# Weights decoded with a scaled copy on ScalarE in place of cleared signs, their factor of two taken out in later steps, and the whole order of steps written anew

## Chip, core and metric

One core of a Trainium2 chip. The metric is the time of one execution of the program in device microseconds; the table below gives the median of the runs shown. Shares of TensorE's clock are shares of 2.4 GHz.

## What is computed

A Nystrom attention of 4 batches with 8 heads (576 positions, 32 landmarks), whose output (2304 tokens by 512) goes through two feed-forward layers:

```
A, Bm, C = softmaxes of q, k and their landmark means
Z = six Newton steps on Bm
x = (A @ Z @ C @ v), heads side by side          # 2304 x 512
h = x @ moe_w_in;  x = (h * tanh(softplus(h))) @ moe_w_out
h = x @ moe2_w_in; x = relu(h) ** 2 @ moe2_w_out
```

All inputs are 4-byte words. As the kernel reads the four weight matrices, each value is a pair of words (`raw` has the shape 128 x 512 x 2): `low` is the lower word of an 8-byte float, `up` the upper one, and the kernel puts a 4-byte float together from them.

## The kernel before, in words

**Order.** The kernel is one long list of steps, `PROGRAM` (2560 steps). A step is `thing.step`, for example `U17.ab`: step `ab` of weight unit 17. The list is walked once and each step issues its instructions; nothing reorders them afterwards, so on every engine and on the queue of SyncE (SP), which issues all transfers, instructions stand in the order of the list. Between engines a tile framework puts the waits, from the order of the list: an instruction waits for earlier steps of the list that use the same tile.

**Weights.** 64 units (`U0` to `U63`, class `Unit`), each a tile of 128 x 512 pairs. Units 0 to 31 are layer 1, 32 to 63 layer 2. The steps of a unit: `d` loads it, `lo` makes a small number of the lower word (ScalarE, L325), `st` puts the sign of the upper word on it (VectorE, L328), `ab` clears the sign of the upper word (L335 on ScalarE for units 0 to 15, L337 on VectorE for units 16 to 63), `cl` clamps and shifts the upper word (VectorE, L341 and L342), `ad` adds both words as integers (GpSimd), `hi` and `lw` split the result in a high and a low part.

**Attention.** Groups `a` to `h` (two for each batch) with small TensorE steps (`tq`, `tk`, `pa`, `pb`, `pc`, `pe`, `pv`), reductions on VectorE (`sq`, `sk`, `cm`, `am`, `su`), exponentials on ScalarE (`ce`, `ae`), and the Newton steps `B0` to `B2` (`be`, `bs`, `n0` to `n5`, `r`, `z`). The steps `F` fold the attention's small matrices into the first weights: `fo` (TensorE, L826), `mh` (ScalarE, L834) and `ml` (VectorE, L837).

**Layer 1.** 24 turns `t0` to `t23`: `f` (matmuls into `h`), `M` (Mish on ScalarE, L893), `c` and `g` (high and low part), `y` (matmuls into `y`), `e` (accumulate). Mish and the exponentials need different function tables of ScalarE; the steps `x.m` and `x.e` load them ahead.

**Layer 2.** Three passes over the tokens. Steps `Q` and `K` work with sums and differences of weight blocks; blocks `Y10` to `Y22` do products into tiles `O` (L841 to L843) and `a` adds them to `total` (L1140 on ScalarE, L1143 on VectorE).

**The end.** The last pass ends with the products of `Q26` and `Q27`: step `yk` (k = 0 to 5; 6 matmuls, L1288 to L1290) adds to one half of a two-bank PSUM tile, and step `Z2.ek` reads that half on VectorE, adds `total` (L1189, two instructions) and writes an output tile. `Z2.ok` issues its four transfers on SP (L1195). `Z2.u4`, `u6`, `u7`, `u8` combine totals (L1163).

```
sums[p, k // 2] = big(f"O{p}{k // 2}", ...)     # one tile [2, 512] for k and k + 1
ps = sums[p, k // 2][:, k % 2, :]               # Q.y writes, Z2.e reads this half
```

So `y0` and `y1` share a tile, `y2` and `y3`, and `y4` and `y5`.

Of the kernel before, what the change touches and what calls it, by code (L numbers as in the profile page):

```python
# [29 lines left out]
BOTTOM = 2.0 ** -15  # L30
TOP = 122880.0 - 2.0 ** -7
NW = 24
BESIDE = 64
# [20 lines left out]
    B0.n2@at+2 U3.ab U2.cl f.lk B0.r2 c.Sk c.tl@y B0.z2 U3.cl c.TL d.tk@h a.tb U3.ad a.cv U7.ab b.pv@y+1 d.sk d.lv
    b.ae U2.ad a.ah c.pb@at B0.n3@y+2 c.PB d.Tk c.pc@h U7.cl c.lv B0.r3 d.Sk B0.z3 b.cr U7.ad B0.n4@y c.cm b.cv
    e.tk@h B0.r4 a.al B0.z4 c.ce b.su B0.n5@y d.tl@y d.TL c.pa@at e.lv B0.z5 U7.hi B0.pw@y+3 e.Tk c.at U7.lw d.pb@y
    c.am U5.lo d.pc@at b.mu U4.hi B0.wz d.cm F00.fo@h U4.lw b.tb d.ce e.sq b.ah d.pe@at b.al U8.d F00.mh f.tk@h+4
    f.lv d.PB d.ET F00.ml c.mi U6.lo f.lq d.pa@at B1.bx t0.f0 c.ae d.at B1.be f.Tk U6.st t0.f1 c.su U6.ab t0.f2
    t0.M0 B1.bs t0.f3 d.cr U5.st B1.nr@y t0.M1 B1.rs c.pe@h U8.lo d.pv@y U5.ab d.am B1.n0@y+2 U6.cl f.tq@at B1.z0
    U8.st e.Sq U6.ad d.cv B1.r0 c.ET e.sk B1.n1@y t0.c0 B1.z1 U6.hi B1.r1 t0.g0 e.tq@h B1.n2@y t0.c1 B1.z2 e.Sk d.mi  # L60
    U5.cl B1.r2 U5.ad f.Tq B1.n3@y+4 c.cr c.pv@y e.Tq B1.r3 U5.hi B1.z3 U6.lw B1.n4@y+3 U5.lw c.cv f.sq e.tl@y B1.r4
    e.TL U8.ab B1.z4 f.Sq B1.n5@at B1.z5 t0.g1 e.pc@h U8.cl U8.ad U11.d e.pb@at c.mu d.ae e.PB B1.pw@y B1.wz f.sk
    t0.y0 e.cm f.Sk t0.y1 d.su t0.e0 U11.lo U11.st U9.d f.tl@at f.TL t0.e1 t0.y2 c.tb e.ce f.pa@at f.pc@h F10.fo@h
# [1325 lines left out]
```

## Time and profile before

| | |
|---|---|
| median of 3 runs | 796.35 us (795.89 to 798.09) |
| the profiled execution | 795.44 us |
| its span, first to last instruction | 793.6 us |
| busy: TensorE matmul / VectorE / ScalarE / GpSimd | 764.7 / 588.1 / 367.5 / 384.4 us |
| mean granted TensorE clock | 0.995 |

The span is what the trace shows; 1.84 us of the execution lie around it. A busy TensorE counts overlapped matmuls as one stretch. Step names don't stand in the trace: an instruction there has its line and its tiles, and the step follows from the order of the list (`q26w` and `q27w` are the weights of `Q26` and `Q27`).

### The profile page before, as it was taken

The numbers are of one execution on the slowest core, as the hardware profiler recorded it, in microseconds if no ns is written. First come the engines' busy times: TensorE is split into PE (matmuls) and PEld (weight loads), VectorE is DVE, ScalarE is ACT, GpSimd is POOL, SyncE is SP. The second block draws the span as 40 slices with busy tenths as digits, with TensorE's granted clock in tenths as the row PEclk, the third lists the DMA queues.
The fourth block names the chain that finished last, engine by engine and source line by source line (L and its number), as shares of the span: only waits on it lengthen the run. The fifth ranks groups of instructions, "written<-read, shape, count | busy, mean of one in ns | idle before, by whom it ended". The sixth has DMA issues, their size and how long they took to land.

```text
span 793.6 us, 15301 instructions
## 1 busy us (share of the span) xinstructions
PE 764.7 (96%) x5878; PEld 713.0 (90%) x5878; DVE 588.1 (74%) x937; ACT 367.5 (46%) x582; POOL 384.4 (48%) x273
## 2 busy tenths in 40 slices
PE   5798999999999999999999999999999999999996
PEld 4567989889999999899998988999899999999995
DVE  7998876768557667878777777757776777875883
ACT  5686988744453654556456234240253432232220
POOL 1244445141142543434466657576586587454440
PEclk9999999999999999999999999999999999999999
DMA  9972552223131246564558789888899877779903
GB/s 272 304 202 55 144 172 91 71 54 90 45 99 61 86 171 210 196 232 157 189 207 263 243 276 304 254 269 272 254 289 382 300 251 238 221 217 314 333 33 79
DMA packets 87783, 156.71 MB, mean 197 GB/s; under 512 B 9376, under 2 KB 37024, under 8 KB 87712
## 3 DMA queue, kind: packets, MB, share of 16 engines
q1 hardware_dynamic: 87712, 155.75, 61.9%
q8 instruction: 46, 0.75, 0.4%
q14 instruction: 25, 0.20, 0.1%
HBM read 119.54 MB, written 36.18 MB: 196 GB/s over the span
## 4 chain that ended last, share of the span: by engine, by line
PE 87%; DVE 6%; DMA 2%; ACT 1%; issue 1%; POOL 0%; SPq 0%; DVEq 0%; POOLq 0%; ACTq 0%
PE y L841 8%; PE y L843 8%; PE y L842 8%; PE P L1221 7%; PE P L1222 7%; PE P L1223 7%; PE O L843 4%; PE O L842 4%; PE O L841 4%; PE h L841 4%; PE h L843 4%; PE h L842 4%; PE O L1290 3%; PE O L1289 3%; PE O L1288 3%; PE m L826 2%
## 5 line engine op out<-in xcount | busy, mean ns | idle before, releaser
L1117 POOL TENSOR_TENSOR glr<-A,ghr 128x768 fp32r<-128x768 f32 x49 | 100.1, 2063 | 69.9 <-ACT ghr L1112 69.9
L843 PE MATMUL O<-b,glr 128*128 128x256 f32 x294 | 83.0, 282 | 0.0
L842 PE MATMUL O<-b,ghr 128*128 128x256 f32 x294 | 83.0, 282 | 0.0
L841 PE MATMUL O<-b,ghr 128*128 128x256 f32 x294 | 82.9, 282 | 0.0
L841 PE MATMUL h<-ah,mh 128*128 128x384 f32 (+1 forms) x256 | 78.5, 307 | 0.0
L843 PE MATMUL h<-ah,ml 128*128 128x384 f32 (+1 forms) x256 | 77.9, 304 | 0.0
L842 PE MATMUL h<-al,mh 128*128 128x384 f32 (+1 forms) x256 | 77.9, 304 | 0.0
L955 DVE TENSOR_TENSOR acc<-acc,y 128x384 f32<-128x384 f32 x72 | 39.4, 550 | 51.6 <-PE y L843 51.3
L1112 ACT CAST ghr<-A 128x768 fp32r<-128x768 f32 x49 | 40.1, 837 | 73.8 <-PE O L842 28.0
L1251 DVE TENSOR_TENSOR U<-U,P 128x384 f32<-128x384 f32 x72 | 39.7, 551 | 33.8 <-PE P L1223 32.6
L843 PEld LDWEIGHTS O<-b,glr 128*128 128x128 f32 x294 | 56.1, 191 | 0.0
L842 PEld LDWEIGHTS O<-b,ghr 128*128 128x128 f32 x294 | 56.0, 191 | 0.0
L841 PEld LDWEIGHTS O<-b,ghr 128*128 128x128 f32 x294 | 55.9, 190 | 0.0
L914 DVE TENSOR_TENSOR gl<-s,gh 128x768 fp32r<-128x768 f32 x48 | 48.8, 1019 | 6.8 <-ACT gh L904 6.8
L893 ACT ACTIVATE s<-h 128x768 f32<-128x768 f32 x48 | 38.8, 811 | 31.5 <-PE h L843 21.1
L841 PEld LDWEIGHTS h<-ah,mh 128*128 128x128 f32 x256 | 48.5, 190 | 3.4 <-issue 1.9
L843 PEld LDWEIGHTS h<-ah,ml 128*128 128x128 f32 x256 | 48.6, 190 | 0.0
L842 PEld LDWEIGHTS h<-al,mh 128*128 128x128 f32 x256 | 48.6, 190 | 0.0
L1231 ACT COPY U<-P 128x384 f32<-128x384 f32 x24 | 11.5, 479 | 72.9 <-PE P L1223 70.7
L1251 DVE TENSOR_TENSOR A<-U,P 128x384 f32<-128x384 f32 x56 | 30.2, 549 | 20.1 <-PE P L1223 16.9
L904 ACT CAST gh<-s 128x768 fp32r<-128x768 f32 x48 | 39.7, 835 | 7.2 <-PE y L843 7.0
L348 POOL TENSOR_TENSOR wi<-rawwi 128x512 int32<-128x512 int32 x16 | 18.3, 1145 | 46.7 <-DVE rawwi L342 29.4
(698 smaller groups left out, 2510.2 us busy)
## 6 DMA issues: line engine op xcount, KB each, us to landing
b<-sc SPq DMA_DIRECT2D x98, 256.0 KB, 4.2
rawwo<-in_moe_w_out_dram SPq DMA_DIRECT2D x32, 512.0 KB, 4.2
rawwi<-in_moe_w_in_dram SPq DMA_DIRECT2D x48, 256.0 KB, 4.0
v<-in_v_dram SPq DMA_DIRECT2D x16, 288.0 KB, 7.4
out_dram<-o SPq DMA_DIRECT2D x72, 64.0 KB, 2.7
rawwi<-in_moe_w_in_dram SPq DMA_DIRECT2D x8, 512.0 KB, 4.4
st<-wh SPq DMA_DIRECT2D x8, 512.0 KB, 4.0
st<-ws SPq DMA_DIRECT2D x8, 512.0 KB, 3.0
```

The source lines that it names most:

```text
L841: nc.tensor.matmul(ps, wh, rh, start=start, stop=False)
L842: nc.tensor.matmul(ps, wh, rl, start=False, stop=False)
L843: nc.tensor.matmul(ps, wl, rh, start=False, stop=stop)
L904: nc.scalar.copy(gh, s)
L914: nc.vector.tensor_tensor(self.gl[:, sl, :], self.s[hf], self.gh[:, sl, :].bitcast(F32), ALU.subtract)
L955: nc.vector.tensor_tensor(a, a, ps, ALU.add)
L1112: nc.scalar.copy(self.form(k)[0], self.A[self.src(k)])
L1117: nc.gpsimd.tensor_tensor(lo, self.A[self.src(k)], hi.bitcast(F32), ALU.subtract)
L1221: nc.tensor.matmul(ps[:, :TT], wh[:, c], xh[:, c, :], start=c == 0, stop=False)
L1222: nc.tensor.matmul(ps[:, :TT], wh[:, c], xl[:, c, :], start=False, stop=False)
L1223: nc.tensor.matmul(ps[:, :TT], wl[:, c], xh[:, c, :], start=False, stop=c == 1)
L1251: nc.vector.tensor_tensor(to, x, self.ps[i][:, :TT], ALU.add)
```

## The change

- `ab` becomes one ScalarE instruction for all 64 units: a copy of the upper word, read as a float, times 2^-112. It keeps the sign. The VectorE form (L337) is gone, and so is the sign-clearing function of L335.
- `lo` writes an integer now (scale 2^-29, bias 2^23); `st` is as before; `cl` clamps from above and from below, then shifts, with the same two instructions and other constants.
- The weights come out with a factor of two. It is taken out where a result leaves PSUM: `mh` and `ml` multiply by 0.5; in layer 2 `a`, `f`, `e` multiply by 2^-5. ScalarE copies get a scale; VectorE's two-input adds and subtractions become `scalar_tensor_tensor`, and a VectorE copy becomes a `tensor_scalar`. No instruction is added by that.
- `PROGRAM` has the same 2560 steps in another order from its 54th step on. Its head up to there is the same.

```
 def lo(self):
-    nc.scalar.activation(self.low.bitcast(F32), self.low, AF.Copy, scale=2.0 ** -51, bias=2.0)
+    nc.scalar.activation(self.low.bitcast(I32), self.low, AF.Copy, scale=2.0 ** -29, bias=WHOLE)
 def ab(self):
-    if not self.beside:
-        nc.scalar.activation(self.up.bitcast(F32), self.up.bitcast(F32), AF.Abs)
-    else:
-        nc.vector.tensor_scalar(self.up, self.up, 0x7FFFFFFF, None, ALU.bitwise_and)
+    nc.scalar.activation(self.up.bitcast(F32), self.up.bitcast(F32), AF.Copy, scale=REBIAS)
 def cl(self):
-    nc.vector.tensor_scalar(up.bitcast(F32), up.bitcast(F32), BOTTOM, TOP, ALU.max, ALU.min)
+    nc.vector.tensor_scalar(up.bitcast(F32), up.bitcast(F32), TOP, -TOP, ALU.min, ALU.max)
     nc.vector.tensor_scalar(up, up, 3, None, ALU.logical_shift_left)
 class Fold: mh, ml
-    nc.scalar.copy(self.m[0], self.ps)
+    nc.scalar.activation(self.m[0], self.ps, AF.Copy, scale=0.5)
-    nc.vector.tensor_tensor(self.m[1], self.ps, self.m[0].bitcast(F32), ALU.subtract)
+    nc.vector.scalar_tensor_tensor(self.m[1], self.ps, 0.5, self.m[0].bitcast(F32), ALU.mult, ALU.subtract)
 class Block: a
-    nc.vector.tensor_tensor(t, t, self.ps[k], ALU.add)
+    nc.vector.scalar_tensor_tensor(t, self.ps[k], UNDO, t, ALU.mult, ALU.add)
 class Ending: e
-    nc.vector.tensor_tensor(self.t[h, c][:, ds], x[:, c, :], ps[:, ds], ALU.add)
+    nc.vector.scalar_tensor_tensor(self.t[h, c][:, ds], ps[:, ds], UNDO, x[:, c, :], ALU.mult, ALU.add)
...
 PROGRAM, its end
-    Y22.p5@h Y22.a7 Q26.y4 Q26.y2 (with Q26.h0, Q26.g0, Q27.h0 and others between)
-    Y22.p3@h Z2.u2 Q27.g0 Q27.y4 Z2.u3 Y22.a3 Q26.y0 Q26.y3 Q27.y2 Z2.u7 Q27.y0 Q27.y3 Q26.y1 Z2.u8 Z2.e4 Z2.u4 Z2.o4
-    Z2.u6 Z2.e2 Z2.e0 Q27.y1 Z2.o2 Z2.o0 Z2.e3 Z2.o3 Q26.y5 Z2.e1 Z2.o1 Q27.y5 Z2.e5 Z2.o5
+    Y22.p3@h Z2.u5 Q26.y4 Q27.b3 Y22.a3 Q26.y2 Q27.b1 Q27.y4 Q27.y2 Q26.y0 Q27.y0 Q26.y1 Q26.y3 Q27.y1 Q27.y3 Q26.y5 Q27.y5
+    Z2.u4 Z2.u7 Z2.u8 Z2.e4 Z2.o4 Z2.u6 Z2.e2 Z2.e0 Z2.o0 Z2.o2 Z2.e1 Z2.o1 Z2.e3 Z2.o3 Z2.e5 Z2.o5
```

The first line of the old end is told in words where other steps stand between; the others are the list's own.

## Rows read from the trace of the kernel before

**Rows 1.** The page: busy time of each engine

```profile
PE 764.7 (96%) x5878; PEld 713.0 (90%) x5878; DVE 588.1 (74%) x937; ACT 367.5 (46%) x582; POOL 384.4 (48%) x273
```

**Rows 2.** Windows: width, busy us of PE, PEld, DVE, ACT, POOL, then clock and DMA

```profile
10.00:80.00 70.00, 57.02 (x914) 44.42 (x922) 64.05 (x139) 50.41 (x110) 28.19 (x26) 0.98 0.72 200
80.00:160.00 80.00, 79.07 (x1005) 71.25 (x988) 57.53 (x111) 63.97 (x109) 29.35 (x26) 1.00 0.40 118
160.00:420.00 260.00, 259.88 (x1709) 247.04 (x1708) 186.33 (x300) 129.80 (x184) 107.15 (x76) 1.00 0.43 139
420.00:780.00 360.00, 357.79 (x2217) 341.67 (x2216) 271.42 (x378) 119.62 (x177) 218.41 (x136) 1.00 0.80 259
780.00:787.50 7.50, 6.64 (x28) 4.80 (x26) 2.92 (x8) 0.00 (x0) 0.00 (x0) 1.00 0.39 95
```

**Rows 3.** Timeline of TensorE, last products: start us, us, instruction [idle before, releaser]

```profile
780.48 0.39 PE L1290 MATMUL O<-q27w,gl 128*128 128x512 f32 x1
...
781.84 0.39 PE L1290 MATMUL O<-q26w,gl 128*128 128x512 f32 x1
783.07 0.50 PE L1288 MATMUL O<-q27w,gh 128*128 128x512 f32 x1 [0.84 <-DVE o L1189]
...
787.10 0.39 PE L1290 MATMUL O<-q27w,gl 128*128 128x512 f32 x1
```

**Rows 4.** TensorE's waits after 80 us: total, times, longest

```profile
PE P L1221 <- DVE C L1251: 0.9, 1, 0.9
PE O L1288 <- DVE o L1189: 0.8, 1, 0.8
PE O L1290 <- DVE gl L1274: 0.6, 1, 0.6
```

**Rows 5.** Timeline of VectorE, 777 us to the end

```profile
776.73 0.96 DVE L1163 TENSOR_TENSOR sum<-sum,sum 128x768 f32<-128x768 f32 x1
780.91 0.75 DVE L1189 TENSOR_TENSOR o<-sum,O 128x256 f32<-128x256 f32 x2 [3.22 <-PE O L1290]
782.26 1.42 DVE L1189 TENSOR_TENSOR o<-sum,O 128x256 f32<-128x256 f32 x4 [0.61 <-PE O L1290]
784.78 0.75 DVE L1189 TENSOR_TENSOR o<-sum,O 128x256 f32<-128x256 f32 x2 [1.10 <-PE O L1290]
787.52 0.75 DVE L1189 TENSOR_TENSOR o<-sum,O 128x256 f32<-128x256 f32 x2 [1.99 <-PE O L1290]
```

**Rows 6.** Timeline of the SP queue, 781 us to the end

```profile
781.69 9.26 SPq L1195 DMA_DIRECT2D out_dram<-o  x20
```

**Rows 7.** Groups by line and shape: busy us, mean ns, idle before

```profile
L337 DVE TENSOR_SCALAR rawwo<-rawwo 128x512 uint32<-128x512 uint32 x24 | 13.6, 578 | 0.1
L337 DVE TENSOR_SCALAR rawwi<-rawwi 128x512 uint32<-128x512 uint32 x24 | 11.3, 477 | 0.2
...
L325 ACT ACTIVATE rawwo<-rawwo 128x512 f32<-128x512 uint32 x32 | 21.7, 679 | 28.8 <-DMA rawwo<-in_moe_w_out_dram 28.8
L335 ACT ACT_TABLE_LOAD x3 | 3.8, 1283 | 0.1
...
L1143 DVE TENSOR_TENSOR sum<-sum,O 128x768 f32<-128x768 f32 x32 | 30.3, 948 | 9.0 <-PE O L843 8.9
L1089 DVE SCALAR_TENSOR_TENSOR A<-A 128x768 f32<-128x768 f32 x28 | 33.6, 1226 | 0.1
```

**Rows 8.** Timeline of VectorE ahead of L1221's wait for L1251

```profile
425.61 0.76 DVE L337 TENSOR_SCALAR rawwo<-rawwo 128x512 uint32<-128x512 uint32 x2
```

**Rows 9.** First pass's end: VectorE and ScalarE reading halves of one tile

```profile
569.31 0.69 DVE L1299 COPY o<-O 128x512 f32<-128x512 f32 x1 [1.81 <-PE O L1290]
570.03 0.59 ACT L1299 COPY o<-O 128x512 f32<-128x512 f32 x1 [3.60 <-DVE o L1299]
...
574.43 0.69 DVE L1299 COPY o<-O 128x512 f32<-128x512 f32 x1
575.21 0.59 ACT L1299 COPY o<-O 128x512 f32<-128x512 f32 x1 [4.58 <-DVE o L1299]
```

More of the change, by code (lines that the diff above doesn't have):

```diff
@@ L29 @@
 N_NEWTON = 6
-BOTTOM = 2.0 ** -15
-TOP = 122880.0 - 2.0 ** -7
 NW = 24
-BESIDE = 64
+REBIAS = 2.0 ** -112
+WHOLE = 2.0 ** 23
+TOP = 2.0 ** -96 * (1.75 - 2.0 ** -22)
+UNDO = 2.0 ** -5
 NQ = 8
@@ L54 @@
[L54 to L63, printed above, removed]
@@ L189 @@
-    Y21.b12 Z1.o4 Y20.b8 Y21.h2 Q24.d1 Y20.l6 Q24.p6 Q24.d2 Q24.p7 Y21.b13 Q25.a3 Y20.b9 Q24.p4 Q26.a0 Q24.d3 Q25.a4
-    Y20.a5 Y21.l2 Q24.p3 Y21.h0 Y20.l4 Z1.o5 Q25.a5 Y21.b6 Y21.b0 Y20.p3@h Q24.d6 Y20.a2 Z1.o0 Y21.h1 Y21.t1 Q26.a2
-    Q24.p5 Y21.b2 Z1.o2 Y21.p4@h Y21.l0 Q24.d4 Q24.d5 Q25.p1 Q25.s Q24.d7 Q25.a1 Y21.b7 Y21.b9 Y21.t3 Y21.h5 Q26.a4
-    Y20.p6@at Y21.a4 Y20.a3 Y21.h3 Y21.b10 Q25.p2 Y21.b3 Y21.b8 Y21.l1 Q26.a3 Q25.p6 Q26.a5 Y21.l3 Y21.b11 Q26.a1
-    Y21.t2 Q25.d1 Q25.p7 Q25.d2 Q25.p5 Q25.d3 Y21.p1@h Q26.a6 Q25.d4 Y22.b12 Y21.t4 Q25.d5 Y22.b1 Y22.b0 Q26.p1
@@ L194 @@
-    Q26.s Y21.p5@h Q25.p4 Y22.r3 Y22.r0 Y22.b8 Q26.b1 Q26.p2 Q26.d1 Y20.a6 Y21.p2@at Q25.p3 Y21.l5 Y21.h4 Q27.a4
-    Y21.h6 Y21.a5 Q25.d6 Q26.p6 Q27.a0 Y21.l6 Q25.d7 Y22.h0 Q27.a2 Y21.p7@h Y21.a1 Y22.h2 Y22.r2 Q26.p7 Y21.l4
-    Y22.r1 Y21.b5 Y22.h1 Y21.b4 Y22.b3 Q26.d2 Q26.d3 Q26.p5 Y22.l1 Q26.p4 Y21.a2 Y22.l0 Y22.b2 Y21.p6@at Q26.d4
-    Q26.b3 Q27.a3 Q26.d5 Q27.a5 Y22.l2 Q26.p3 Q26.d6 Y21.a6 Y22.b13 Q26.d7 Y22.b7 Y22.t1 Q27.a6 Q27.a1 Y22.p1@h
-    Q26.b0 Y22.t3 Y22.a1 Y21.a7 Y22.b10 Y22.h3 Y22.l3 Y22.t2 Q27.p1 Q27.s Q27.p2 Y22.b9 Y22.b5 Y22.b11 Y22.b4
@@ L199 @@
-    Y21.p3@h Y22.h5 Y22.h4 Y22.p2@at Y22.b6 Y22.t4 Q26.b2 Q27.d1 Y22.l4 Q26.r1 Q26.r0 Q27.p6 Y22.l5 Y22.p4@h Q27.d2
-    Q27.b2 Y22.a2 Y22.a4 Q27.p7 Q27.d3 Y21.a3 Q27.p4 Y22.h6 Q27.p5 Z2.u5 Q27.d4 Q27.b1 Q26.h1 Q27.d5 Q27.d6
-    Y22.p6@at Q27.p3 Q27.r1 Y22.a6 Y22.p7@h Q27.d7 Q27.r0 Q27.h1 Y22.l6 Q26.g1 Y22.a7 Q26.h0 Q26.g0 Y22.p5@h Q26.y4
-    Q26.y2 Q27.h0 Y22.a5 Q27.b0 Q27.b3 Q27.g1 Y22.p3@h Z2.u2 Q27.g0 Q27.y4 Z2.u3 Y22.a3 Q26.y0 Q26.y3 Q27.y2 Z2.u7
-    Q27.y0 Q27.y3 Q26.y1 Z2.u8 Z2.e4 Z2.u4 Z2.o4 Z2.u6 Z2.e2 Z2.e0 Q27.y1 Z2.o2 Z2.o0 Z2.e3 Z2.o3 Q26.y5 Z2.e1 Z2.o1
@@ L204 @@
-    Q27.y5 Z2.e5 Z2.o5
+    b.tq@h b.sq U1.ab U0.ab c.lq a.pe@at U1.cl b.Sq b.Tq d.sq b.tl@y U1.ad U3.d@m U2.lo b.TL a.cr U0.cl b.pc@h+4
+    a.ET U4.lo b.pb@at b.PB a.ae b.pa@at U2.st a.lv U4.st B0.bx b.cm U4.ab B0.be b.lv b.at c.tk@h+3 B0.bs U4.cl b.ce
+    B0.nr@y d.lk U7.lo c.Tk U6.d@gh U2.ab e.lk B0.rs a.su b.pe@h b.am b.ET U7.st c.tq@at+2 c.sq c.Tq c.Sq B0.n0@at+5
+    a.pv@y b.mi U3.lo B0.r0 B0.z0 B0.n1@y a.mu c.sk U3.st B0.r1 U3.ab B0.z1 d.tq@h c.Sk a.cv d.Sq U7.ab B0.n2@at+2
+    d.tk@h B0.r2 U2.cl c.tl@y e.lq B0.z2 d.Tq U3.cl U5.d c.TL f.lk B0.n3@y+2 d.sk c.lv B0.r3 c.pb@at a.tb d.Tk U0.ad
@@ new lines @@
+    U7.cl U4.ad b.ae B0.z3 U3.ad c.PB U2.ad b.pv@y+1 a.ah c.pc@h B0.n4@y b.cr c.pa@at c.cm B0.r4 U7.ad b.cv B0.z4
+    e.tk@h c.ce b.su d.Sk B0.n5@y B0.z5 d.tl@y B0.pw@y+3 U4.hi d.TL U7.hi c.at a.al B0.wz c.am d.pc@at U5.lo d.pb@y
+    e.Tk U4.lw b.mu d.cm d.PB U6.lo d.lv b.tb d.ce e.sq c.mi U7.lw F00.fo@h f.tk@h+4 F00.mh F00.ml d.pe@at b.ah d.ET
+    b.al U8.d d.pa@at c.ae t0.f0 B1.bx B1.be c.su B1.bs U5.st d.at f.Tk f.lq U6.st t0.f1 e.Sq t0.f2 t0.M0 U6.ab
+    B1.nr@y U5.ab d.pv@y B1.rs U8.lo t0.f3 t0.c0 B1.n0@y+2 d.am U6.cl U6.ad B1.z0 B1.r0 f.tq@at d.cr B1.n1@y e.sk
@@ new lines @@
+    t15.M0 t13.e0 W1.l0 t15.f2 U40.ab t13.y2 U40.cl t14.c1 W1.sv0 t13.y3 t13.e2 U40.ad U42.d t15.f3 t16.f0 t14.g1
+    t14.y0 t15.c0 t13.e3 U41.ad W2.v0 W2.h0 t14.y1 W2.v1 U43.d W2.v3 W2.v2 W2.l0 x.m t15.M1 t16.f1 U42.lo U42.st
+    U43.lo t15.g0 t14.e1 F03.fo@at W2.sv0 U42.ab U43.st U43.ab t14.y2 t14.e0 U42.cl t14.y3 t14.e3 U43.cl t16.f2
+    t15.c1 W2.h1 U42.ad t16.M0 t14.e2 t15.g1 W2.l1 U48.d U48.lo t16.f3 t15.y0 U43.ad W2.sv1 W3.h0 t17.f0 U48.st
+    W3.v0 U48.ab t17.f1 F03.mh t15.y1 U48.cl U49.d t16.c0 t15.e0 t16.M1 W3.v2 t17.f2 t16.c1 U48.ad F03.ml t16.g0
@@ new lines @@
+    W7.l0 K0.h1 t23.f1 U39.lo X0.l3 t21.e3 t21.e2 U38.ab Q00.a6 W7.sv0 t22.g1 t23.M0 t22.y0 X0.t3 U38.cl W7.l1
+    t23.f2 t23.f3 K0.h0 t23.M1 t22.e0 U39.st Q02.a5 t23.c0 W7.sv1 x.two U39.ab X0.h2 X0.h0 t23.g0 K0.l1 U38.ad
+    t23.c1 U45.d X0.l4 t22.y1 x.e t22.y2 K0.sv1 t22.e1 x.m K0.l0 t22.y3 t23.g1 x.e X0.h6 K0.sv0 t22.e2 U39.cl t23.y0
+    t22.e3 U39.ad U44.d Q01.a2 X0.l0 K1.t1 t23.e0 X0.h5 t23.y1 t23.e1 Q00.a4 K1.t3 X0.l5 t23.y2 U45.lo t23.y3 Q01.a5
+    U44.lo U45.st X0.h1 Q01.a0 Q01.a3 U36.hi X0.l1 t23.e2 Q04.a3 K1.t2 Q00.p1 Q00.s X0.l6 U38.hi Q00.p7@at U44.st
@@ new lines @@
+    Q16.a1 Y12.b13 X2.t2 Q17.s Q16.p2 Y12.b0 Q17.a6 X2.t3 Q17.a4 X2.h4 Y12.b1 Y11.a6 Y12.l2 Y11.p3@h Y12.b7 Y12.b10
+    Q16.d1 Y12.t1 Y12.b6 Q17.p2 Y12.l1 X2.h1 Q16.p6 Y11.a3 Y12.p2@at Q16.d2 Q17.d1 Q16.p7 Y12.l0 Y12.t3 Y12.h3
+    Y12.b11 Q22.a2 Q20.a0 Q16.d3 Q20.a2 Q16.p5 Q16.d4 Q16.p4 X2.h6 Y13.r0 Q17.a1 Y12.l3 Q20.a3 Y12.t2 Q16.d6
+    Y12.p4@h Y12.b8 Y12.b9 X2.h0 Y13.b0 Q17.p6 Q16.d5 Y11.a5 Q17.d2 Y13.h0 Q17.p7 Y13.b1 X2.l6 Y12.b5 Y12.p1@h
+    Y12.a2 Y12.h5 Y13.l0 Q20.a6 X2.h5 Y12.l5 Q20.a4 Q17.p5 Q20.a5 Y12.h4 Y12.a4 X2.l0 Q17.d3 X2.h2 Q16.p3 X2.l1
@@ new lines @@
+    Y21.l2 Q24.p7 Q26.a0 Q24.p4 Q24.d3 Q25.a1 Y21.p4@h Q26.a2 Q24.d6 Q24.p5 Y21.r1 Y20.a7 Q26.a4 Y21.t1 Q24.p3
+    Y21.h0 Y21.b6 Q24.d4 Z1.o4 Y20.l4 Y21.b3 Q24.d5 Y20.p3@h Y21.a4 Y21.h1 Y21.b7 Q26.a5 Y20.p6@at Y21.h3 Y21.b2
+    Y20.a3 Q26.a3 Y21.l1 Z1.o2 Y22.b1 Y21.b11 Z1.o0 Q24.d7 Y21.b10 Q25.p1 Q25.s Q25.p2 Q25.p6 Q26.a6 Y21.t3 Q27.a4
+    Y21.l3 Q26.a1 Q25.d1 Y21.b8 Y21.l0 Q25.d2 Q25.p5 Y20.a6 Q25.p7 Q25.d3 Y21.h5 Y22.r0 Y21.p1@h Y21.b4 Y21.b9
+    Q26.p1 Y21.p5@h Y21.b5 Q27.a2 Q25.d4 Y22.b0 Y21.t2 Q27.a3 Y21.t4 Q25.d5 Q26.s Q27.a0 Q26.p2 Q27.a6 Y22.r3 Y21.h4
@@ new lines @@
+    Q26.p6 Q26.d1 Y22.b13 Y21.a1 Q25.p4 Y21.p2@at Y22.h0 Y21.l4 Q25.d6 Q26.d2 Q25.p3 Y22.h2 Q26.p7 Y22.r2 Y21.l5
+    Q25.d7 Y21.a5 Y21.p7@h Y22.b3 Y22.b12 Y22.r1 Q26.d3 Y21.a2 Q26.p5 Y22.l2 Q26.d4 Q26.p4 Y22.h1 Y22.l0 Y22.t1
+    Y22.b2 Y21.h6 Q26.d5 Q27.a1 Y21.p6@at Y22.b11 Q27.a5 Q26.p3 Y22.p1@h Q26.d6 Q26.b2 Q26.r1 Q27.b0 Y21.l6 Q27.p1
+    Q26.d7 Y21.a7 Y22.h3 Q26.h1 Y22.a1 Y21.a6 Y22.l3 Y22.t3 Y22.t2 Y21.p3@h Y22.l1 Q26.r0 Y22.b8 Q26.h0 Y22.t4
+    Q26.g1 Q27.p2 Y22.b9 Q27.s Y22.b10 Y22.b7 Y22.p4@h Q26.b1 Y22.p2@at Y22.h6 Q26.g0 Y22.b4 Q27.d1 Q27.p6 Y22.a2
@@ L205 @@
+    Q27.p7 Y22.h4 Q27.d2 Q27.d3 Q27.p4 Y22.l6 Y22.l4 Y21.a3 Q27.p5 Y22.h5 Y22.b6 Y22.a4 Y22.p6@at Q27.d4 Q26.b0
+    Q27.d5 Y22.l5 Q27.d6 Y22.a6 Q27.b2 Q27.p3 Y22.b5 Q27.r1 Q27.h1 Q26.b3 Y22.p7@h Q27.d7 Q27.r0 Y22.p5@h Y22.a7
+    Q27.g1 Q27.h0 Q27.g0 Z2.u2 Y22.a5 Z2.u3 Y22.p3@h Z2.u5 Q26.y4 Q27.b3 Y22.a3 Q26.y2 Q27.b1 Q27.y4 Q27.y2 Q26.y0
+    Q27.y0 Q26.y1 Q26.y3 Q27.y1 Q27.y3 Q26.y5 Q27.y5 Z2.u4 Z2.u7 Z2.u8 Z2.e4 Z2.o4 Z2.u6 Z2.e2 Z2.e0 Z2.o0 Z2.o2
+    Z2.e1 Z2.o1 Z2.e3 Z2.o3 Z2.e5 Z2.o5
 """
@@ L297, in __init__ @@
             self.by_rows = kind == "i" and li == 0
-            self.beside, self.uses = False, 0
+            self.uses = 0
         def d(self, tag="raw"):
@@ L1139, in a @@
                 total[p, k] = page(f"sum{p}{k}").rearrange("p a n -> p (a n)").rearrange("p (c n) -> p c n", n=256)
-                nc.scalar.copy(total[p, k], self.ps[k])
+                nc.scalar.activation(total[p, k], self.ps[k], AF.Copy, scale=UNDO)
             else:
                 t = total[p, k]
-                nc.vector.tensor_tensor(t, t, self.ps[k], ALU.add)
+                nc.vector.scalar_tensor_tensor(t, self.ps[k], UNDO, t, ALU.mult, ALU.add)
             give(f"O{self.n}{k}")
@@ L1175, in f @@
                     x, ps = total[self.p, k], self.last.ps[k]
[L1176 removed]
+                    nc.vector.scalar_tensor_tensor(to, ps[:, c, :], -UNDO if k == 4 else UNDO, x[:, c, :], ALU.mult, ALU.add)
             if k == 5:
@@ L1298, in e @@
             outs[p, k] = t = flat(page(f"o{p}{k}"))[:, :DM]
-            (nc.scalar.copy if k % 2 else nc.vector.tensor_copy)(t, sums[p, k // 2][:, k % 2, :])
+            ps = sums[p, k // 2][:, k % 2, :]
+            if k % 2:
+                nc.scalar.activation(t, ps, AF.Copy, scale=UNDO)
+            else:
+                nc.vector.tensor_scalar(t, ps, UNDO, None, ALU.mult)
             if k % 2:
@@ L1347, in nystrom_mish_relu2 @@
     things["x"] = Tables()
-    for u in units[16:BESIDE]:
-        u.beside = True
     with tc.manual_schedule():
```

245 lines of the change are left out of this document (115 added, 130 removed).

## Prediction

> **What bounds the kernel now.** I read the page's busy times first: TensorE is busy 764.7 of 793.6 us, VectorE 588.1, ScalarE 367.5 [rows 1]. Since a share over the whole span mixes stages, the windows come next [rows 2]. They show three stretches. From 10 to 80 us TensorE is busy 57.0 of 70 us and VectorE 64.1: here VectorE has the least slack (6 us), and TensorE waits for it and for ScalarE in turn. From 80 to 780 us TensorE is busy 696.7 of 700 us: the sum of the three rows, so whatever other engines gain there can be worth 3.3 us at most. After 780 us it has 6.6 us of work in 7.5, and then 6.1 us pass without it, from the end of the last matmul (787.10 + 0.39 = 787.5) [rows 3] to 793.6. The list of TensorE's waits after 80 us says what can be given back there: 0.9, 0.8 and 0.6 us are its largest [rows 4].
>
> The end needs a look of its own, for the diff rewrites it. Four `Z2.e` groups of instructions run after 780 us [rows 5], and SP issues 20 transfers without a pause, 9.26 us, from 781.69 to 790.95 [rows 6]. That is 0.463 us for each, 1.85 us for the four of one output tile. The last `e` ends at 787.52 + 0.75 = 788.3, but its four transfers begin only 1.85 us before 790.95, at 789.1. So the end of the kernel hangs on SP's chain, which starts with `e2`, and not on the last matmul. From the chain's end to the span's end it is 793.6 - 790.95 = 2.65 us.
>
> **The change, part by part.**
>
> *`ab`.* VectorE loses 48 instructions, 13.6 + 11.3 = 24.9 us [rows 7]. ScalarE gains 48 at 0.68 us (the row of L325: the same function on a tile of that size), 32.6 us, and goes from 367.5 to 400 of 793.6. Both lie in 80 to 780 us, where TensorE's work covers them. All units whose decoding stands in the stretch bound by VectorE are units 0 to 15, which already had `ab` on ScalarE: there VectorE gets nothing back. What is left is the 0.9 us wait of L1221 for a VectorE sum [rows 4]: some 6 us ahead of it VectorE spends 0.76 us on two `ab` [rows 8], and those are gone. I count -0.8 us for that and nothing for the rest. The bounds are 0 and -3.3 us, the idle time of the windows.
>
> *Tables.* L335 has three table loads of 1.28 us [rows 7]: the sign-clearing function runs with the table of the exponential and not with Mish's. They don't go away. Counted in the list, changes between Mish and the other functions are 25 before and 25 after; where an `ab` brought the table, the next `ae` or `ce` brings it now. Sum: 0.
>
> *Scaled evictions.* ScalarE's copies keep their form. VectorE's become three-operand instructions: 128x768 with both sources in one row is 948 ns for the two-input form from PSUM (L1143) and 1226 ns for the three-operand form from SBUF (L1089) [rows 7]. No row shows the three-operand form with that size from PSUM, so it costs between 0 and 0.28 us more; 32 of L1143 make at most 9 us of VectorE's time in a stretch where it has 89 us idle of 360 [rows 2]. Hidden: 0. I take no extra, for the work per element is the same.
>
> *`lo`, `cl`.* Same instructions with other constants: 0.
>
> *The order, head and body.* In the list's first third VectorE's sequence is almost the same: up to `F00.ml` and up to `t0.g1` the sets of its steps are the same, with neighbours swapped, and later single steps such as `g.sq` and `e.tb` move behind the next turns. I take 0, with 3 us to either side: half of the 6 us that VectorE has idle there [rows 2], and for a loss the same. For the body, 2 us to either side.
>
> *The order of the end.* This is the term that decides. In the list before, each `e` stands between the products. In the new list all twelve `y` of `Q26` and `Q27` come first and then all six `e`. If an `e` only waited for its own half this would cost nothing. The trace says that it waits for the tile. `Z2.e2` reads the half that `Q27.y2` finished; it has no other work ahead of it (VectorE idles 3.22 us) and starts at 780.91, which is the end of `Q27.y3`, 780.48 + 0.39 = 780.87, the product that writes the tile's *other* half and stands before it in the list. `Z2.e0` starts at 782.26, the end of `Q26.y1` (781.84 + 0.39), again the other half. Then `Q27.y1` waits 0.84 us until `e0` is done, though it writes the half that `e0` doesn't read [rows 3, 5]. In the first pass ScalarE's read of one half twice starts just when VectorE's read of the other half ends, 570.03 after 569.31 + 0.69 and 575.21 after 574.43 + 0.69 [rows 9]. Five places, one reading: uses of the two halves follow each other in the list's order.
>
> So in the new list `Z2.e4`, first of the six on VectorE, must wait for `Q27.y5`, which is TensorE's last work. Behind it in VectorE's order stand `u6`, `e2`, `e0`, `e1`, `e3`, `e5`, and SP waits for each of them. With P the new end of TensorE:
>
> - `e4` done at P + 0.8 (0.03 as at 787.52, and 0.75), and SP issues its four, until P + 2.7.
> - `u6` takes 0.9 (0.96 less the overlap), `e2` and `e0` 0.7 each (1.42 for two) [rows 5]: `e0` is done at P + 3.1, and the list has `o0` as the second output. SP starts again there.
> - Its 20 remaining transfers take 9.26 us, until P + 12.4; VectorE's 0.7 for each `e` keeps ahead of SP's 1.85.
> - The end follows 2.65 us later: P + 15.0, where before it was P + 6.1. That is +8.9 us.
> - P itself moves by -0.8, since `Q27.y1` has no `e0` to wait for.
>
> The tile slots of `Q27.b1` and `Q27.b3`, loaded late in the new list, come free with `Y22.p4` and `Q27.p2`, long before; I count no wait for them.
>
> **Sum.** 8.9 - 0.8 (wait at the end) - 0.8 (L1221) + 0 (head, body, tables, evictions) = +7.3 us. On the profiled execution's 795.44 that is 802.7; its median stood 0.9 us higher, 796.35, and there it is 803.6. I take 803.
>
> **Rivals.**
>
> *Halves are free (faster or no change).* Each `e` waits only for its own half. Then `e4` runs while TensorE is still busy, SP's chain starts 9 products of 1.36 us (781.84 - 780.48) before P, and the end is set by `e5`: P + 0.8 + 1.85 + 2.65 = P + 5.3, so -0.8, and with the other two terms -2.4 us: 794.0. Against it stand the five places above. For it: none of them is the tile of `y4` and `y5`. It decides as soon as `e4` starts before `Q27.y5` ends. The Trainium skill's page "PSUM — Partial Sum Buffer", section "PSUM bank collisions raise a hardware error", asks for guards by bank and quadrant; the halves are different banks, so by that rule this rival would hold. The trace differs: a wait of 3.22 us for the other bank.
>
> *The head gives it back.* VectorE's 6 idle us before 80 us are closed by the new order: 803 - 6 = 797. Against it: the same steps precede the first turns, so the bound there has the same work.
>
> *ScalarE becomes late.* Each `ab` takes 0.68 in place of 0.52 us (24.9 over 48), and stands behind Mish and the high parts on ScalarE, whose busy share is 50% from 160 to 420 us and 80% from 80 to 160 [rows 2]. If a tenth of the 32.6 us came through to TensorE it would be +3.3: 806. The Trainium skill's page "ScalarE: Activation LUTs", section "Rules for kernel authors", puts multiplications on VectorE rather than ScalarE, which speaks against this change; the trace agrees on the price of one instruction, 0.52 against 0.68 us. The point is a ScalarE near 95% busy in some stage, which no row from 160 us on is near.
>
> *The change doesn't do what it says* would be an `ab` that still loads tables or runs on VectorE; that would cost nothing at the end and isn't a case of its own.
>
> **Numbers.** Forecast 0.77, halves free 0.09, head 0.07, ScalarE or a stall in the body 0.07. The forecast's own range is 799.5 to 806 (3 us for the head, 2 for the body, not both at once). To hold 8 in 10 I go from 797.5 to 807. A difference of 0.3% (2.4 us) is about what a measurement here can tell from none: faster ends at 794.0, slower begins at 798.7. Faster: half of the halves rival and a little of the head's, 0.06; the same: the rest of the two and the forecast's lower edge, 0.13; slower 0.81.
>
> **What would show it.** Right: no L1189 before the last L1290; a first L1189 that sat idle for several us until it; 24 transfers after TensorE's end, in two runs of 4 and 20; TensorE's end near 786 us and 15 us behind it; L337 gone, 64 instructions of about 0.68 us at the scaled copy; 25 table loads beside the first. Wrong: an L1189 among the last products (the halves are free), or TensorE's end moved by more than 3 us (the head or body weighs more than I allow).

## The result, and the profile after

The changed kernel takes 804.28 us (median of 4 runs, 803.12 to 806.12) where the kernel before took 796.38 (4 runs): a ratio of 1.0100, 95% interval 1.0083 to 1.0117. It is slower, by 7.9 us; forecast were 803.0 and +7.3. Its profiled execution took 804.14 us with a span of 802.1, 8.5 us more than before's 793.6.

The page's busy times of the changed kernel, and under them its windows, with the columns of [rows 1] and [rows 2]:

```profile
PE 764.5 (95%) x5878; PEld 714.0 (89%) x5878; DVE 571.4 (71%) x889; ACT 397.6 (50%) x630; POOL 381.2 (48%) x273
```

```profile
10.00:80.00 70.00, 55.66 (x881) 44.02 (x882) 63.45 (x138) 49.54 (x106) 27.44 (x26) 0.98 0.74 207
80.00:160.00 80.00, 79.29 (x1019) 70.90 (x1019) 58.57 (x110) 65.53 (x115) 29.04 (x26) 1.00 0.36 111
160.00:420.00 260.00, 260.00 (x1716) 247.90 (x1717) 168.95 (x264) 160.13 (x230) 107.02 (x77) 1.00 0.44 143
420.00:780.00 360.00, 357.70 (x2216) 341.53 (x2215) 269.74 (x365) 118.74 (x177) 216.41 (x135) 1.00 0.78 255
780.00:787.50 7.50, 7.44 (x33) 5.82 (x31) 0.03 (x1) 0.00 (x0) 0.00 (x0) 1.00 0.00 0
```

VectorE has 48 instructions and 16.7 us less, ScalarE 48 more and 30.1 us more. TensorE has the same work. From 10 to 80 us it idles 14.34 us in place of 12.98; from 80 us to its end 3.0 in place of 4.1 (each window's width less its busy time). The two nearly cancel: TensorE ends at 787.44, where before it ended at 787.49. All of the loss lies behind that point.

The timelines of the end (line numbers are two lower than before: L1187 is `Z2.e`, L1288 the last matmul of a product, L1193 a transfer). VectorE, then the SP queue (from 788 to 790 us, and from 790 us on), then TensorE's last instruction:

```profile
787.47 0.76 DVE L1187 SCALAR_TENSOR_TENSOR o<-O,sum 128x256 f32<-128x256 f32 x2 [11.76 <-PE O L1288]
788.15 0.95 DVE L1161 TENSOR_TENSOR sum<-sum,sum 128x768 f32<-128x768 f32 x1
789.01 3.40 DVE L1187 SCALAR_TENSOR_TENSOR o<-O,sum 128x256 f32<-128x256 f32 x10
```

```profile
788.26 1.74 SPq L1193 DMA_DIRECT2D out_dram<-o  x4
790.45 9.26 SPq L1193 DMA_DIRECT2D out_dram<-o  x20
```

```profile
787.05 0.39 PE L1288 MATMUL O<-q27w,gl 128*128 128x512 f32 x1
```

Against [rows 5, 6] the picture is plain. Before, `e2` ran at 780.91, between two products. Now VectorE sits idle for 11.76 us and starts its first `e` 0.03 us behind TensorE's last matmul. SP then issues all 24 transfers: the four of `e4` at once, then, behind a pause of 0.45 us in which it waits for `e0`, the other 20 in 9.26 us, 0.463 us each as in [rows 6]. The span ends 2.4 us behind the last one: 14.66 us from TensorE's end to the span's end, where it was 6.1.

The TensorE waits of [rows 4] have gone from their places, and others have come. The second line is L1221's of before under its new line number, but elsewhere: at 745 us, ahead of a product with `q26w`, where before it stood at 432 us, ahead of one with `q01w`.

```profile
PE O L839 <- ACT o L1299: 1.2, 1, 1.2
PE P L1219 <- DVE C L1249: 0.7, 1, 0.7
```

The edits do what they say. These groups of instructions on ScalarE answer to L337 and L335 in [rows 7]: 64 scaled copies of 0.68 us, and no table load at that line. All table loads of the changed kernel are 26, 25 beside the first, as in the kernel before:

```profile
L335 ACT ACTIVATE rawwi<-rawwi 128x512 f32<-128x512 f32 x32 | 21.6, 681 | 12.5 <-DVE rawwi L329 12.4
L335 ACT ACTIVATE rawwo<-rawwo 128x512 f32<-128x512 f32 x32 | 21.5, 681 | 26.2 <-DVE rawwo L329 26.2
```

### The profile page after: what moved, and what is told of

It is laid out like the page before. It is cut to its first block, busy times and chain, and to the rows that moved or that the text cites. A ratio compares the mean times of both kernels' runs of the same rounds, so it can differ in the third digit from the quotient of the medians.

```text
span 802.1 us, 15286 instructions
## 1 busy us (share of the span) xinstructions
PE 764.5 (95%) x5878; PEld 714.0 (89%) x5878; DVE 571.4 (71%) x889; ACT 397.6 (50%) x630; POOL 381.2 (48%) x273
## 4 chain that ended last, share of the span: by engine, by line
PE 86%; DMA 6%; DVE 4%; SPq 1%; issue 1%; ACT 0%; DVEq 0%; ACTq 0%
PE y L839 9%; PE y L841 8%; PE y L840 8%; PE P L1219 7%; PE P L1221 7%; PE P L1220 7%; PE h L839 5%; PE h L841 4%; PE h L840 4%; PE O L839 4%; PE O L841 4%; PE O L840 4%; PE O L1287 3%; PE O L1288 3%; PE O L1286 3%; DMA q<-in_q_dram 3%
## 5 line engine op out<-in xcount | busy, mean ns | idle before, releaser
L1249 DVE TENSOR_TENSOR U<-U,P 128x384 f32<-128x384 f32 x72 | 39.6, 550 | 30.1 <-PE P L1221 29.3
L902 ACT CAST gh<-s 128x768 fp32r<-128x768 f32 x48 | 40.0, 832 | 11.9 <-PE y L841 11.8
```

Source lines behind the costliest of these rows:

```text
L902: nc.scalar.copy(gh, s)
L1249: nc.vector.tensor_tensor(to, x, self.ps[i][:, :TT], ALU.add)
```

## The experiments

Four groups of questions: is the end's order the cause; is the tile the cause of the wait; what do edits and list cost apart; what sets the time behind TensorE's end. Medians of the kernel before, taken beside them, lie between 795.8 and 796.4 us. "P" is again TensorE's end.

### The order of the end, undone

In the changed kernel, only the end of the list is altered: each `e` stands behind the product that completes its half, ahead of the next product on that tile.

```
-... Q27.y4 Q27.y2 Q26.y0 Q27.y0 Q26.y1 Q26.y3 Q27.y1 Q27.y3 Q26.y5 Q27.y5 Z2.u4 Z2.u7 Z2.u8 Z2.e4 Z2.o4 ...
+... Q27.y4 Z2.u4 Z2.u7 Z2.u8 Z2.e4 Z2.o4 Z2.u6 Q27.y2 Z2.e2 Z2.o2 Q26.y0 Q27.y0 Q26.y1 Z2.e0 Z2.o0 Q26.y3
+    Q27.y1 Z2.e1 Z2.o1 Q27.y3 Z2.e3 Z2.o3 Q26.y5 Q27.y5 Z2.e5 Z2.o5
```

> The changed kernel with one thing altered: at the end of the list each Z2.e and its transfers stand again between the products, behind the product that completes their half and ahead of the next that writes the other half. Theory (an e waits for the whole tile, and SP's 24 transfers start behind it): e4 and e2 run before TensorE's last work, SP's transfers spread over the last products, and the span ends 0.8 + 1.85 + 2.65 = 5.3 us behind TensorE's end in place of 14.65: 804.3 - 9.4 = about 795 us. Rival (the loss comes from the decoding, the scaled evictions or the order of the head and body): TensorE's end moves, the stretch behind it counts little, and the time stays within 2 us of 804.

Measured: 794.97 us (12 runs), 9.3 less than the changed kernel, and a ratio to the kernel before of 0.9981 (0.9969 to 0.9994). The end of VectorE's timeline:

```profile
776.61 0.74 DVE L1181 SCALAR_TENSOR_TENSOR o<-O,sum 128x256 f32<-128x256 f32 x2
...
788.46 0.76 DVE L1181 SCALAR_TENSOR_TENSOR o<-O,sum 128x256 f32<-128x256 f32 x2 [1.96 <-PE O L1282]
```

The first `e` now runs 11.8 us ahead of P (788.42), and only the last one behind it. The span ends 4.9 us behind P. The loss was the end's order.

### The same order in the kernel before

```
-Z2.u7 Q27.y0 Q27.y3 Q26.y1 Z2.u8 Z2.e4 Z2.u4 Z2.o4 Z2.u6 Z2.e2 Z2.e0 Q27.y1 Z2.o2 Z2.o0 Z2.e3 Z2.o3 Q26.y5 ...
+Q27.y0 Q27.y3 Q26.y1 Q27.y1 Q26.y5 Q27.y5 Z2.u7 Z2.u8 Z2.e4 Z2.o4 Z2.u4 Z2.u6 Z2.e2 Z2.e0 Z2.o0 Z2.o2 ...
```

> The kernel before with one thing altered: the six Z2.e of the end, the sums ahead of them and their transfers stand behind all products, in the order that the changed kernel has. Theory (tile wait and SP's chain): about 15 us behind TensorE's end in place of 6.1, with TensorE's end 0.8 us earlier: 796.4 + 8 = about 804 us. Rival (it takes the changed edits to make the loss): 796, within 1 us.

Measured: 804.09 us, ratio 1.0102 (1.0083 to 1.0121). VectorE and SP at the end, with P at 788.42:

```profile
788.46 0.75 DVE L1183 TENSOR_TENSOR o<-sum,O 128x256 f32<-128x256 f32 x2 [11.18 <-PE O L1284]
```

```profile
789.24 12.42 SPq L1189 DMA_DIRECT2D out_dram<-o  x24
```

The same idle stretch and the same 24 transfers, with the old decoding and two-input evictions. SP's 12.42 us hold a pause of 1.4 us behind the first four, since the sums `u4` and `u6` stand ahead of `e2` here. The order makes the loss without the edits. One part of the expectation missed: P should have come 0.8 us earlier, and in this execution, the slowest of four (806.24 us), it came 0.9 later.

### The same order, with other tiles

The changed kernel with its list untouched; in the last pass `y3` and `y5` get tiles of one bank of their own.

```
+if p == 2 and k in (3, 5):
+    if first:
+        sums[p, k, "own"] = one(f"O{p}own{k}", "y")
+    ps = sums[p, k, "own"]
...
```

> The changed kernel with its order untouched, and only the tiles of PSUM altered: in the last pass the sums of y3 and y5 lie in tiles of one bank of their own, so that e4, e2, e3 and e5 each read a tile that no later product writes; e0 and e1 still share one. Theory (the wait is for the tile): e4 runs at the end of Q27.y4, nine products before TensorE's end, SP's 24 transfers start there, and the span ends 5 to 9 us behind TensorE's end in place of 14.65: 795 to 799 us. Rival (an e waits for whatever product stands before it in the list, whichever tile it writes): the first L1187 still starts at TensorE's end, and the time stays at 804.

Measured: 798.07 us (10 runs), 6.2 less than the changed kernel. VectorE's timeline, with P at 787.63:

```profile
775.82 0.74 DVE L1190 SCALAR_TENSOR_TENSOR o<-O,sum 128x256 f32<-128x256 f32 x2
...
777.35 0.74 DVE L1190 SCALAR_TENSOR_TENSOR o<-O,sum 128x256 f32<-128x256 f32 x2
783.58 1.41 DVE L1190 SCALAR_TENSOR_TENSOR o<-O,sum 128x256 f32<-128x256 f32 x4 [5.49 <-PE O L1296]
784.94 0.76 DVE L1190 SCALAR_TENSOR_TENSOR o<-O2own,sum 128x256 f32<-128x256 f32 x2
787.66 0.76 DVE L1190 SCALAR_TENSOR_TENSOR o<-O2own,sum 128x256 f32<-128x256 f32 x2 [1.96 <-PE O2own L1296]
```

`e4` and `e2`, whose tiles no later product writes, run 12 and 10 us ahead of P though they stand behind all products in the list. `e0`, which still shares a tile with `y1`, waits 5.49 us for the last product of `y1`. So an `e` waits for what stands before it in the list and writes its *tile*; neither its own half alone counts, nor everything ahead of it.

### The edits under the old list

The changed code, with the whole list of the kernel before.

```
-PROGRAM = (the changed list)
+PROGRAM = (the list of the kernel before)
```

> The changed decoding, evictions and scaling with the whole list of the kernel before. The prediction's terms for the edits alone: -0.8 us for the wait of L1221 and 0 for tables and evictions, so 795.6 us, between 794 and 796.5. Rival (ScalarE becomes late, or the three-operand evictions cost time): up to 3 us slower, 799. With the first run of this group it says whether the order of head and body moved TensorE's end: TensorE's end there against its end here.

Measured: 803.28 us, ratio 1.0082 (1.0063 to 1.0100). This is neither the prediction's term nor within the rival's 3 us: the edits that I had priced at about nothing cost 7.0 us in this list. TensorE's waits after 80 us (total, times, longest) say where to look, and the timelines of VectorE, ScalarE and TensorE around 350 us show it:

```profile
PE y L833 <- DVE acc L947: 4.2, 2, 3.0
```

```profile
349.19 0.68 DVE L323 SCALAR_TENSOR_TENSOR rawwi<-rawwi 128x512 uint32<-128x512 uint32 x1
356.51 0.43 DVE L333 TENSOR_SCALAR rawwi<-rawwi 128x512 f32<-128x512 f32 x1 [6.64 <-ACT rawwi L329]
...
357.65 0.55 DVE L947 TENSOR_TENSOR acc<-acc,y 128x384 f32<-128x384 f32 x1
```

```profile
352.17 0.81 ACT L885 ACTIVATE s<-h 128x768 f32<-128x768 f32 x1 [3.23 <-PE h L835]
352.88 1.02 ACT L826 ACTIVATE mh<-m 128x1024 fp32r<-128x1024 f32 x1
353.90 1.28 ACT L1312 ACT_TABLE_LOAD   x1
...
355.31 1.18 ACT L329 ACTIVATE rawwi<-rawwi 128x512 f32<-128x512 f32 x2
```

```profile
358.25 0.44 PE L833 MATMUL y<-gh,wo_12h 128*128 128x384 f32 x1 [3.01 <-DVE acc L947]
...
360.01 0.52 PE L833 MATMUL y<-gh,wo_14h 128*128 128x384 f32 x1
...
364.11 0.33 PE L833 MATMUL y<-gh,wo_12h 128*128 128x384 f32 x1
```

Start from the last of these timelines. TensorE waits 3.01 us for a VectorE sum (L947). That sum takes 0.55 us, but stands in VectorE's order behind a clamp (L333), which waits 6.64 us for two `ab` on ScalarE (L329). They take 1.18 us together, but stand in ScalarE's order behind a Mish (L885), which itself waits 3.23 us for TensorE, and behind an eviction and a table load. In the kernel before, those two `ab` ran on VectorE directly ahead of the clamp, and none of this was in their way:

```profile
347.78 0.76 DVE L337 TENSOR_SCALAR rawwi<-rawwi 128x512 uint32<-128x512 uint32 x2
348.57 0.43 DVE L341 TENSOR_SCALAR rawwi<-rawwi 128x512 f32<-128x512 f32 x1
```

ScalarE is not short of time: in the window from 160 to 420 us of this run it is busy 150.5 of 260. What counts is what stands ahead in its queue.

The wait has a second price. Windows of the same run around it:

```profile
352.00:356.00 4.00, 3.24 (x19) 2.92 (x18) 0.00 (x0) 3.82 (x6) 0.00 (x0) 1.00 0.00 0
356.00:360.00 4.00, 1.75 (x6) 1.75 (x7) 3.42 (x8) 3.97 (x6) 1.63 (x2) 0.83 0.03 8
360.00:364.00 4.00, 4.00 (x19) 4.00 (x19) 2.62 (x5) 0.50 (x2) 0.50 (x1) 0.74 0.69 209
364.00:368.00 4.00, 4.00 (x25) 4.00 (x24) 3.54 (x5) 3.53 (x6) 2.43 (x1) 1.00 0.51 189
```

Behind the idle 3.01 us the granted clock is 0.83 and 0.74, part of the time on its lower level (1.2 GHz); ahead of it, it was 1.00. From 358.25 to 364.11 us TensorE starts 24 matmuls of one shape in 5.86 us. The next 12, at full clock, take 2.08 us (364.11 to 366.19), so 24 would take 4.16. That is 1.7 us lost beside the wait, 4.7 in all.

This run also tests a term of the prediction. Of L1221's waits (L1213 here), the one of [rows 4] ahead of a product with `q01w` is still there, as long as before:

```profile
439.13 0.44 PE L1213 MATMUL P<-fh,q01w 128*128 128x384 f32 x1 [0.86 <-DVE C L1243]
```

The `ab` that I held for its cause are gone from VectorE in this run, and the wait isn't.

### One place of it

The same kernel (changed code, old list) with three steps moved:

```
-t19.f3 t19.M1 Q02.a2 U56.st F23.mh x.e U57.ab U56.ab t19.c0
+t19.f3 U56.st U57.ab U56.ab t19.M1 Q02.a2 F23.mh x.e t19.c0
```

> The changed edits with the whole list of the kernel before, but one place altered: the shift-and-join step of unit 56 and the multiplications of units 57 and 56 stand ahead of t19's Mish on ScalarE in place of behind it and the Exp table load. Theory A: VectorE's idle stretch of 6.64 us ahead of a clamp and TensorE's wait of 3.0 us behind it go, the other waits stay: 803.3 - 3.0 = about 800.3 us. Rival B (the wait of 3.0 us is not from ScalarE's order): it stays, or moves to another place, 803.

Measured: 798.56 us, 4.7 less than with the steps where they were; I had expected 3.0, for the wait alone. The waits of TensorE show the 3.0 us gone, and the second of the two still there:

```profile
PE y L833 <- DVE acc L947: 1.2, 1, 1.2
```

The granted clock is 1.00 in every window from 346 to 368 us of this run. Wait and clock together, 4.7 us by the rows above, are what came back. Three steps in 2560 carry two thirds of what the edits cost in the old list.

### The multiplication on VectorE

Again the old list with the changed code, but `ab` of units 16 to 63 on VectorE:

```
+if not self.beside:
     nc.scalar.activation(self.up.bitcast(F32), self.up.bitcast(F32), AF.Copy, scale=REBIAS)
+else:
+    nc.vector.tensor_scalar(self.up.bitcast(F32), self.up.bitcast(F32), REBIAS, None, ALU.mult)
```

> The changed edits with the whole list of the kernel before (the run that took 803.3 us), but the multiplication of units 16 to 63 on VectorE, where the clearing of signs had been, as a multiplication by the same constant. Theory A (in the old list a VectorE clamp that had its ab ahead of it on its own engine must now wait for ScalarE, whose queue stands still behind a Mish that waits for TensorE; the sums queued behind the clamp come late, and TensorE waits for them): the waits of 3.0 us and 1.2 us for a VectorE sum go, and the time is 796 us, within 1. Rival B (the three-operand evictions or the scaled copies cost it): stays at 803.

Measured: 796.37 us (10 runs), ratio 1.0008 (0.9998 to 1.0019). Of the waits of 3.0 and 1.2 us for a VectorE sum, 0.2 us is left. With the engine back where it was, all the other edits (new constants, scaled copies, three-operand evictions) cost nothing that can be measured. The 7.0 us are the move to ScalarE alone.

### The old code under the new list

The kernel before with the list of the first experiment.

```
-PROGRAM = (the list of the kernel before)
+PROGRAM = (the list of the first experiment)
```

> The code of the kernel before, with its sign-clearing on VectorE, under the changed list of head and body and the interleaved end (the list of the first run). With the changed edits this list took 795.0 us, the old list with the old edits 796.3, the old list with the changed edits 803.3. If the new order of head and body only repairs what the edits break: 796, within 1. If the order gains by itself: 795 or less. If the two need each other both ways (each list fits its own edits): 798 or more.

Measured: 802.66 us, ratio 1.0088 (1.0074 to 1.0102). The third case holds: each list fits its own edits. One reason is a new one. The kernel before has 26 table loads on ScalarE; here there are 32, of which the sign-clearing function (L329) has six in place of three:

```profile
L329 ACT ACT_TABLE_LOAD x6 | 7.7, 1283 | 0.1
```

What one of them looks like in ScalarE's timeline:

```profile
57.34 1.28 ACT L887 ACT_TABLE_LOAD   x1
58.64 0.81 ACT L887 ACTIVATE s<-h 128x768 f32<-128x768 f32 x1
59.47 1.28 ACT L329 ACT_TABLE_LOAD   x1
60.76 1.23 ACT L329 ACTIVATE rawwo<-rawwo 128x512 f32<-128x512 f32 x2
...
64.55 1.28 ACT L887 ACT_TABLE_LOAD   x1
```

The new list puts a Mish, an `ab` and a Mish in a row. With the scaled copy that is one table; with the sign-clearing function it is three loads. The Trainium skill's page "ScalarE: Activation LUTs", section "Table sets: the hidden batching unit", counts that function among the cheap ones that every set holds, by which there would be no load here; the trace differs, with six loads of 1.28 us at its line.

### New list, no sign-clearing, multiplication on VectorE

The list of the first experiment with the code that has scaled copies on ScalarE for units 0 to 15 and VectorE's multiplication for the others.

```
-PROGRAM = (the list of the kernel before)
+PROGRAM = (the list of the first experiment)
```

> The new list with the interleaved end (795.0 us with the changed edits, 802.7 with the old code), and the changed edits but for units 16 to 63, whose multiplication runs on VectorE. It stands between these two: units 0 to 15 use the scaled copy on ScalarE, which needs no table of its own. Theory T (under the new list the old code loses by the sign-clearing function's six table loads between 59 and 124 us, and TensorE is 5 us late by 136 us): those loads go, the loss of the rest (2.3 us) stays, about 797.5 us. Rival V (the old code loses by VectorE's 25 us more work in the body): 802, with TensorE late only behind 136 us.

Measured: 798.50 us, ratio 1.0038 (1.0023 to 1.0052). Windows from 10 to 136 us of three kernels under the same list, first the changed code, then the old code, then this one, each in its own fence:

```profile
10.00:136.00 126.00, 112.24 (x1441) 95.52 (x1442) 105.67 (x199) 97.15 (x187) 54.15 (x49) 0.97 0.60 173
```

```profile
10.00:136.00 126.00, 107.73 (x1408) 89.84 (x1409) 104.69 (x197) 101.28 (x186) 50.12 (x45) 0.97 0.56 166
```

```profile
10.00:136.00 126.00, 113.23 (x1444) 96.25 (x1444) 105.62 (x199) 97.17 (x188) 54.23 (x49) 0.99 0.59 173
```

The old code's TensorE has done 33 matmuls less than the changed code's by 136 us, and 4.5 us less work; without the table loads the deficit is gone. Of the 7.7 us between the medians of the old and the changed code under this list, 4.2 go with the sign-clearing function's loads (and the rest of the old code, which cost nothing measurable under the old list), and 3.5 are left with VectorE's `ab` in a list made without them. By P of the single profiled executions (795.72, 790.40 and 788.42 us) the parts are 5.3 and 2.0, so the division is known to a microsecond or so. Theory T holds; its 797.5 was 1.0 us low.

### What sets the time behind TensorE's end

The changed kernel, its order untouched, with the transfers of the last pass shared between two queues:

```
-nc.sync.dma_start(
+(nc.scalar if self.p == 2 and m % 2 else nc.sync).dma_start(
```

> The changed kernel with its order untouched, and in the last pass every second transfer of an output tile issued by ScalarE's queue in place of SP's. Theory (behind TensorE's end the price of the late e's is the 24 issues of SP, 11.45 us): with 12 on each queue VectorE's chain becomes the bound (0.8 + 0.9 + five e of 0.7 = 5.2 us behind TensorE's end), the last two issues 0.9 and 2.4 to the end: 8.5 us in place of 14.65, about 798 us. Rival (the transfers or VectorE set the end, not the issues): 803 to 804.

Measured: 799.96 us, 4.3 less than the changed kernel, where about 6 were expected. SP's queue, up to 789 us and from there on, then ScalarE's from 789 us on:

```profile
787.67 0.80 SPq L1193 DMA_DIRECT2D out_dram<-o  x2
789.86 5.04 SPq L1193 DMA_DIRECT2D out_dram<-o  x10
```

```profile
789.86 5.14 ACTq L1193 DMA_DIRECT2D out_dram<-o  x10
```

From P (786.85) to the span's end it is 10.75 us in place of 14.66. The direction is the theory's: issuing on one queue was the bound. The size isn't. Both queues stand still for 1.4 us behind the first output tile, until `e0` is done; there VectorE is the bound. Then each issues ten transfers in 5.04 and 5.14 us, 0.50 to 0.51 us each, where SP alone took 0.463. I had counted 0.46 each and only the last two of a queue behind VectorE's last `e`. But ten on each queue are left when `e0` is done, and VectorE's last `e` ends at 791.82, 3 us ahead of the last issue. SP's list of waits also has 0.8 us, in three places, for earlier transfers, of which the changed kernel's has none.

### The interleaved end on two queues

The changed code with the first experiment's list, and the transfers of the last pass on two queues.

```
-nc.sync.dma_start(
+(nc.scalar if self.p == 2 and m % 2 else nc.sync).dma_start(
```

> The changed kernel with the interleaved end of the first run, and in the last pass every second transfer of an output tile issued by ScalarE's queue in place of SP's. The first run's span ends 4.9 us behind TensorE's end: 0.8 for the last e, 1.75 for SP's four issues, 2.35 to the span's end. If an issue takes SP 0.46 us and ScalarE no more, the last four take 0.9: -0.9 us, 794.1 us, and both kernels are beaten. If the transfers themselves set the end: 795.0 as before.

Measured: 794.12 us (11 runs), 0.85 less than with one queue (the expectation was 0.9); ratio to the kernel before 0.9976 (0.9963 to 0.9989). The span ends 4.2 us behind P in place of 4.9. It beats the changed kernel by 10 us and the kernel before by 2.2. What the second queue adds is not clear of the noise: the intervals of the two ratios, 0.9963 to 0.9989 here and 0.9969 to 0.9994 with one queue, overlap for the most part.

## Why the prediction was right, and where only its sum was

**The end, +8.9.** Right in mechanism and nearly in size: P + 14.66 where I had P + 15.0, so +8.6. The idle VectorE, the first `e` at P and the 24 issues in runs of 4 and 20 came as written. SP starts again at P + 3.0 (predicted 3.1), and its 20 take the predicted 9.26 us, until P + 12.3 (12.4). Most of the 0.3 us that are missing stand behind the last issue: 2.39 us to the span's end in place of 2.65. Undoing the order, making it in the old kernel and separating the tiles each moved the time as the theory said, by -9.3, +7.8 and -6.2 us. The rival "halves are free" is dead: the Trainium skill's rule on banks ("PSUM — Partial Sum Buffer", section "PSUM bank collisions raise a hardware error") does not describe what this kernel waits for, an 11.76 us wait for the other half's product in the changed kernel.

**TensorE's end, -1.6.** Not there: P moved by 0.05 us. The waits of L1288 and L1221 that I named did go, and TensorE idles 1.1 us less after 80 us; but new waits of 1.2 and 0.7 us came, and the head lost 1.4. This is within the 3 us that I had allowed the head, and it is the term by which the sum was short: 7.3 predicted, 7.9 between the medians, 8.5 between the profiled spans. P is read from one execution of each kernel; the first experiment, whose list is the same up to the last products, ended at 788.42, a microsecond later. The reason for L1221's 0.8 us was incomplete as well: with `ab` gone from VectorE under the old list, that wait kept its 0.86 us, and with the old code under the new list a wait of 0.83 us for the same line stands ahead of a product with `q02w`. It took both to be rid of it.

**Edits 0, head and body 0.** Here the sum was right and the reasons were not: that it came out is luck. The two zeros stood for themselves: the edits hidden "where TensorE's work covers them", the order neutral because "the sets of its steps are the same". The four combinations of code and list say otherwise:

| | list of before | new list, end interleaved |
|---|---|---|
| code of before | 796.3 | 802.7 |
| changed code | 803.3 | 795.0 |

The edits alone cost 7.0 us, the list alone 6.4; together they are 1.4 us faster than before, and most of that is the interleaved end (4.9 us behind P in place of 6.1). The failed step is the one on `ab`: I added up VectorE's saving and ScalarE's cost as busy time, found both covered by TensorE, and took "nothing for the rest". The cost is not in busy time. It is a hop to another engine's queue: a clamp that used to follow its `ab` on the same engine waits for whatever stands ahead of the `ab` over there.

**The rival "ScalarE becomes late".** It was the true mechanism of the edits, with a wrong condition and a low price. I let it decide at "a ScalarE near 95% busy"; it happened at 58% (150.5 of 260 us). I priced it at 3.3 us; in the old list it cost 7.0, of which 1.7 are the clock behind one 3.01 us wait. That the forecast didn't need it is owed to the new list, under which no such wait is left: in the changed kernel TensorE is busy 260.00 of 260 us from 160 to 420, where the old list with the same code has 255.80.

**Tables 0, evictions 0, `lo` and `cl` 0.** Right. 25 loads beside the first in both kernels, and VectorE's 32 additions into the sums from PSUM average 951 ns, against the two-input form's 948 [rows 7]: the lower of my two bounds. That the tables balance holds for each list with its own code only, as the old code under the new list shows with 32 loads.
